# Twelve idle bf16 products around the diagonals in attention's first two turns

## The chip, the cores and the metric

One core of one Trainium2 chip runs the whole program in one launch. The metric is the time on the device in microseconds, the median of several executions. A profiled execution is a further one, with its own time.

## The reference

Three stages follow one another, all in float32:

```
for t in range(S):                       # attention, per batch b and head h
    cur   = (u * k[t]) outer v[t]
    y[t]  = r[t] @ (state + cur)
    state = w[t][:, None] * state + k[t] outer v[t]
x   = y as [1536 tokens, 384]
x   = each token's best expert of 8 (softmax weight, relu(x @ w1[e]) @ w2[e])
out = (silu(x @ w_gate) * (x @ w_val)) @ w_out
```

Batch 2, 8 heads, 768 steps, head size 48; experts 384 to 1024 to 384; the last stage 384 to 1536 to 384.

## The kernel before, in words

Attention is done in chunks of 128 tokens, 12 in all (NU), six for each batch. The loop `for u in range(NU - 2)` at L851 is one turn for each chunk. The program order is written by hand: each engine takes its instructions in the order in which the loop issues them, so what stands ahead on an engine's queue delays what stands behind. For a chunk, VectorE makes scaled keys and queries (prep1 and prep2; tile M at L410 and L413, and rk at L417), TensorE makes the scores (L451), the transposed keys (kgtok, L462), the values y (L474 and L478) and the state's increment (L490), ScalarE copies the results out of PSUM (L453 the scores, L464 the transposed keys as kgt, L509 the state as Sb, L543 the transposed rows and diagonals as xT), and GpSimd masks the scores (L454) and forms the diagonal's part of the output (own, L431). VectorE adds that part to y as x (L515).

In turn u, TensorE's order is: state(u); in turns 0 and 1 some idle products (`warm`); scores(u + 1); kgtok(u + 1); gate_t(u - 1), which has the diagonals and the transposes of the finished chunk's rows; values(u). In turns 0 and 1 gate_t calls `diag`, products with only two moving columns: those of chunks 0 and 1 in turn 0, those of chunk 2 in turn 1. An f32 product counts twice in the profile, so turn 0 has 16 such records and turn 1 has 8. From turn 2 on, the diagonals are made in another form (L531).

`warm(n, pool, tag)` at L435 issues n products of a 128x128 matrix of ones with 512 columns in bf16, to a PSUM buffer of that pool and tag; nobody reads the result. The pool ps1 has one buffer for each tag: "xT" is also gate_t's, "T" is also the buffer of kgtok's transposes (psT), which ScalarE copies out at L464. A new tile of a tag waits until the old one's readers are done. Calls of warm stand ahead of the first scores (12 products), after the first kgtok (4), in turn 0 (8) and in turn 1 (4) ahead of the scores, and at the end of attention (1 and 2).

After the last turns, the tokens are sorted to experts, the first expert's input is formed on TensorE (L795) and the experts begin (L1226, L1244), followed by the last stage (L1337, L1360).

Of the kernel before, what the change touches and what calls it, by code (L numbers as in the profile page):

```python
# [41 lines left out]
def build(tc, cap, dm, tk, vt, ub, cst, wg, w1, w2, wgate, wval, wout, out):  # L42
# [257 lines left out]
    ps1 = at.enter_context(tc.tile_pool(name="ps1", bufs=1, space=PSUM))  # L300
# [51 lines left out]
    def prep1(u):  # L352


        if u >= NU:
            return
        W = dmt[u % 3][:, 0:2 * NP * XW].rearrange("p (h a j) -> p h a j", h=2, a=NP)
        Xf[u] = ap3.tile([128, 2 * (NP * XW + G + 1)], F32, tag="X", name="X")
        X = Xt[u] = halved(Xf[u], XW)
        for h in range(2):  # L360
            nc.vector.tensor_tensor_scan(out=run(X[:, h], h), data0=run(W[:, h], h), data1=run(xinit[:, h], h),
                                         initial=0.0, op0=ALU.mult, op1=ALU.max)
            tick()
        A = halved(anch[u % 2], HC)
        for h in range(2):
            nc.vector.reciprocal(out=anchors(A, h, G - 1), in_=anchors(X, h, G + 1))
            tick()
# [20 lines left out]
    def prep0(u):  # L388

        if u >= NU:  # L390
            return
        W = dmt[u % 3][:, 0:2 * NP * XW].rearrange("p (h a j) -> p h a j", h=2, a=NP)
        m = wm[u % 2].rearrange("p h a (g j) -> p h a g j", j=G)
        w8 = [W[:, h, :, 2 * h:2 * h + HC].rearrange("p a (g j) -> p a g j", j=G) for h in range(2)]
        nc.scalar.copy(out=m[:, 0, :, :, 1:G], in_=w8[0][:, :, :, 0:G - 1])
        nc.scalar.copy(out=m[:, 1, :, :, 0:G - 1], in_=w8[1][:, :, :, 1:G])
# [23 lines left out]
    def diag(u, ps):  # L420

        rk = rkt.pop(u).rearrange("p a s j -> p a (s j)")
        for p in range(NP):
            nc.tensor.matmul(ps[:, 2 * p:2 * p + 2], rk[:, p, :], ud[:, p, E + 2 * p:E + 2 * p + 2], start=True, stop=True)
# [10 lines left out]
    def warm(n, ps=None, tag="T"):  # L435

        ps = (ps or psA).tile([128, 512], F32, tag=tag if ps else "A0", name="psW")
        x = xinit.rearrange("p h a j -> p (h a j)").bitcast(BF16)[:, 0:512]
        for _ in range(n):
            nc.tensor.matmul(ps, ones, x, start=True, stop=True)  # L440

    def scores(u):
        if u >= NU:
            return
        M = Mt[u]
        sb = At[u] = ap2.tile([128, 2, NP, C], F32, tag="A", name="A")
        ps = [psA.tile([128, 512], F32, tag=f"A{g}", name="psA").rearrange("p (a t) -> p a t", a=NP) for g in range(2)]
        for p in range(NP):
            for g in range(2):
                h = M[64 * g:64 * g + 64, p].rearrange("p (x s) b -> p x (s b)", x=2)  # L450
                nc.tensor.matmul(ps[g][:, p], h[:, 0], h[:, 1], start=True, stop=True)  # L451
        for g in range(2):
            nc.scalar.copy(out=sb[:, g], in_=ps[g])  # L453
            nc.gpsimd.affine_select(out=sb[:, g], in_=sb[:, g], pattern=[[0, NP], [1, C]], base=0,  # L454
                                    channel_multiplier=-1, compare_op=ALU.is_gt, fill=0.0)

    def kgtok(u):
        if u < NU and (u + 1) % UPB:
            M = Mt[u]
            pst = ps1.tile([128, NP, C], F32, tag="T", name="psT")  # L460
            for p in range(NP):
                nc.tensor.transpose(pst[:, p, :], M[:, p, 0:2, :].rearrange("p a b -> p (a b)"), ident)  # L462
            kgt[u] = ap2.tile([128, NP, C], F32, tag="kgt", name="kgt")
            nc.scalar.copy(out=kgt[u], in_=pst)  # L464
# [16 lines left out]
    def state(u):  # L481

        if not (u + 1) % UPB:
            return
        P = ps1.tile([128, NP, D], F32, tag="P", name="psP")
        k = kgt.pop(u)
        for p in range(NP):
            for g in range(2):
                c0 = D * (2 * p + g)
                nc.tensor.matmul(P[64 * g:64 * g + 64, p, :], k[:, p, 64 * g:64 * g + 64], vts[u][:, c0:c0 + D],  # L490
                                 start=True, stop=True, skip_group_check=True)
        d = ap2.tile([128, NP], F32, tag="d", name="d")
        nc.vector.tensor_tensor(out=d, in0=Xt[u][:, 1, :, XW - 1], in1=Xt[u + 1][:, 0, :, 0], op=ALU.mult)
        tick()
        src = P
        if u % UPB:
            src = ap2.tile([128, NP, D], F32, tag="Sa", name="Sa")
            nc.vector.tensor_tensor(out=src, in0=P, in1=Sc[u], op=ALU.add)
            tick()
        s = Sc[u + 1] = ap2.tile([128, NP, D], F32, tag="Sc", name="Sc")  # L500
        nc.vector.tensor_tensor(out=s, in0=src, in1=d.unsqueeze(2).to_broadcast([128, NP, D]), op=ALU.mult)
        tick()

    def expand(u):
        if not (u + 1) % UPB:
            return
        s = Sc[u + 1]
        for g in range(2):
            nc.scalar.copy(out=Sb[(u + 1) % 2][64 * g:64 * g + 64, :, D * g:D * g + D], in_=s[64 * g:64 * g + 64])  # L509

    def xrow(u):
        if u < 0:
            return
        x = xt[u] = gp.tile([128, DM], F32, tag="x", name="x", bufs=7)
        nc.vector.tensor_tensor(out=x, in0=yt.pop(u), in1=av.pop(u), op=ALU.add)  # L515
        tick()
# [3 lines left out]
    def gate_t(u, qs=(), rows=()):  # L520


        if u < 0 and not qs:
            return
        ps = ps1.tile([128, 4 * C], F32, tag="T" if u == NU - 1 else "xT", name="psx")
        if rows:
            w, q = rows
            rk = rkt.pop(q).rearrange("p a s j -> p a (s j)")
            todo = [(wgs[:, k, :], xgt[w][:, k, :]) for k in range(3)] + [(ud[:, p, :], rk[:, p, :]) for p in range(NP)]
            for i, (a, b) in enumerate(todo):  # L530
                nc.tensor.matmul(ps[0:2 * E, DM:DM + C], a, b, start=not i, stop=i == len(todo) - 1, skip_group_check=True)  # L531
            gss[u] = gp.tile([2 * E, C], F32, tag="gs", name="gs")
        w = DM + len(qs) * H
        for i, q in enumerate(qs):
            diag(q, ps[:, DM + i * H:])
        for k in range(3 * (u >= 0)):
            nc.tensor.transpose(ps[:, 128 * k:128 * k + 128], xt[u][:, 128 * k:128 * k + 128], ident)
        xT = gp.tile([128, DM + 2 * H], F32, tag="xT", name="xT", bufs=3)
        c0 = 0 if u >= 0 else DM
        if rows:  # L540
            nc.scalar.copy(out=gss[u], in_=ps[0:2 * E, DM:DM + C])
            w = DM
        nc.scalar.copy(out=xT[:, c0:w], in_=ps[:, c0:w])  # L543
        xgt[u] = xT[:, 0:DM].rearrange("p (k c) -> p k c", k=3)
        for i, q in enumerate(qs):
            a8s[q] = xT[:, DM + i * H:DM + i * H + H]
# [169 lines left out]
    def zero(n):  # L716
        for _ in range(min(n, len(zsteps))):
            c, d = zsteps.pop(0)
            nc.sync.dma_start(out=zv[:, c:d], in_=zrow[:, 0:d - c])
# [131 lines left out]
    for u in range(NU - 2):  # L851
        chosen, counted = ended.get(u - 2), ended.get(u - 3)
        xrow(u - 1)
        state(u)
        if u:
            prep0(u + 2)
        if u < 2:
            warm(8 - 4 * u, ps1, "xT")
        scores(u + 1)
        expand(u)  # L860
        kgtok(u + 1)
        if u:
            prep1(u + 2)
        if u >= 2:
            gate_t(u - 1, rows=(u - 2, u + 1))
        else:
            gate_t(u - 1, ((0, 1), (2,))[u])
            if not u:
                own(0)
            own(u + 1)  # L870
        load_dm(u + 4)
        zero(NZ)
        if counted:
            count(counted)
            place(counted)
            ready += counted
        prep2(u + 2)
        if not u:
            check(1)
            nc.vector.tensor_copy(out=tri, in_=before)  # L880
        check(u + 2)
        values(u)
        if u >= 2:
            columns(u - 1, u - 2, u + 1)
            own(u + 1)
        if chosen:
            flush()
            choose(chosen)
        load_v(u + 3)
        if u >= 4:  # L890
            load_raws(2 * (u - 4) + 1)
        if u >= 5:
            fill(0.0)
        for _ in range(2):
            if ready and not steps:
                scatter(ready.pop(0))
# [583 lines left out]
```

## Time and profile before

| what | value |
|---|---|
| median of 3 runs | 479.93 us (479.17 to 482.4) |
| profiled execution | 482.81 us |
| its span, first to last instruction | 481.1 us |
| mean granted TensorE clock in it | 0.974 |
| TensorE / VectorE / ScalarE / GpSimd busy | 97% / 70% / 50% / 15% |

A row of the timeline gives the start, the duration from the first to the last of the merged instructions, the engine, the line, the operation, what is written and read, and the count; in brackets the idle time ahead of it and what ended it. Products overlap at their ends, so the time from one group's start to the next group's start is what a group costs. PE is TensorE's products, PEld its loading of weights, DVE VectorE, ACT ScalarE, POOL GpSimd.

### The profile page before, as it was taken

The numbers are of one execution on the slowest core, as the hardware profiler recorded it, in microseconds if no ns is written. First come the engines' busy times: TensorE is split into PE (matmuls) and PEld (weight loads), VectorE is DVE, ScalarE is ACT, GpSimd is POOL, SyncE is SP. The second block draws the span as 40 slices with busy tenths as digits, with TensorE's granted clock in tenths as the row PEclk, the third lists the DMA queues.
The fourth block names the chain that finished last, engine by engine and source line by source line (L and its number), as shares of the span: only waits on it lengthen the run. The fifth ranks groups of instructions, "written<-read, shape, count | busy, mean of one in ns | idle before, by whom it ended". The sixth has DMA issues, their size and how long they took to land.

```text
span 481.1 us, 8717 instructions
## 1 busy us (share of the span) xinstructions
PE 468.9 (97%) x3268; PEld 423.9 (88%) x3271; DVE 337.4 (70%) x723; ACT 240.8 (50%) x567; POOL 71.7 (15%) x88
## 2 busy tenths in 40 slices
PE   7999999998999999999999999999999999999994
PEld 3798888898999999999998888888888888888884
DVE  8999899756888685568868968475758677433231
ACT  4466666545787677656545454444534434222220
POOL 3343426531000000000000171000000000003033
PEclk9899989958999999999999999999999999999999
DMA  7899994642779964324524244133100000001011
GB/s 239 196 278 257 341 246 154 213 163 74 251 262 376 329 222 146 123 67 138 193 65 118 81 67 68 65 70 128 32 36 1 0 1 0 1 0 65 2 66 65
DMA packets 33647, 62.53 MB, mean 130 GB/s; under 512 B 5216, under 2 KB 16992, under 8 KB 33600
## 3 DMA queue, kind: packets, MB, share of 16 engines
q1 hardware_dynamic: 31680, 57.20, 39.5%
q0 software_dynamic: 1920, 4.73, 2.7%
q8 instruction: 26, 0.43, 0.4%
q14 instruction: 21, 0.17, 0.1%
HBM read 52.48 MB, written 9.44 MB: 129 GB/s over the span
## 4 chain that ended last, share of the span: by engine, by line
PE 72%; issue 2%; POOL 1%; DVE 0%; POOLq 0%
PE psg L1337 31%; PE psu L1360 14%; PE psh L1226 14%; PE pso L1244 13%; POOL out L1372 1%; PE psx L1211 1%; DVE acc L1370 0%; POOLq L1476 0%; POOLq L1372 0%
## 5 line engine op out<-in xcount | busy, mean ns | idle before, releaser
L1337 PE MATMUL psg<-yb,wu 128*128 128x512 f32 x648 | 156.3, 395 | 0.0
L1337 PEld LDWEIGHTS psg<-yb,wu 128*128 128x128 f32 x648 | 121.3, 188 | 26.2
L1360 PE MATMUL psu<-wu,a 128*128 128x384 f32 x432 | 80.8, 336 | 0.0
L1360 PEld LDWEIGHTS psu<-wu,a 128*128 128x128 f32 x432 | 76.4, 188 | 2.9
L1226 PE MATMUL psh<-xe,wu 128*128 128x240 f32 x576 | 69.1, 277 | 1.6 <-ACTq L1165 1.6
L1226 PEld LDWEIGHTS psh<-xe,wu 128*128 128x128 f32 x576 | 66.2, 190 | 1.9 <-ACTq L1165 1.8
L1244 PE MATMUL pso<-h,wu 128*128 128x240 f32 x576 | 66.4, 275 | 0.0
L1244 PEld LDWEIGHTS pso<-h,wu 128*128 128x128 f32 x576 | 65.3, 189 | 0.0
L211 DVE TENSOR_TENSOR wu<-raw,wu 128x512 fp32r<-128x512 f32 x96 | 62.1, 687 | 1.0 <-DVEq L1165 1.0
L1344 DVE TENSOR_TENSOR t<-t,psg 128x512 f32<-128x512 f32 x36 | 24.7, 686 | 52.6 <-PE psg L1337 35.6
L206 ACT CAST wu<-raw 128x512 fp32r<-128x512 f32 x96 | 55.1, 621 | 3.9 <-PE pso L1244 1.8
L1349 ACT CAST a<-t 128x512 fp32r<-128x512 f32 x36 | 22.3, 619 | 58.1 <-DVE t L1344 58.1
L1233 DVE SCALAR_TENSOR_TENSOR h<-psh,h 128x240 fp32r<-128x240 f32 x64 | 25.1, 403 | 22.8 <-ACT h L1232 22.4
L206 ACT CAST wu<-bits 128x384 fp32r<-128x384 f32 x36 | 18.0, 514 | 40.0 <-DVE bits L199 40.0
L1372 POOL DMA_INDIRECT out<-acc,idc x12 | 11.7, 974 | 174.1 <-DVE acc L1370 172.3
L1259 POOL DMA_INDIRECT idl<-ids,dests x12 | 13.5, 1121 | 161.4 <-DVE bits L186 158.0
L1343 ACT ACTIVATE t<-psg 128x512 f32<-128x512 f32 x36 | 21.5, 596 | 27.5 <-PE psg L1337 27.5
L1350 DVE TENSOR_TENSOR a<-t,a 128x512 fp32r<-128x512 f32 x36 | 24.8, 689 | 11.7 <-ACT a L1349 11.7
L478 PE MATMUL y<-v,A 128*128 128x48 f32 x192 | 28.4, 278 | 0.0
L1232 ACT ACTIVATE h<-psh 128x240 fp32r<-128x240 f32 x64 | 23.2, 373 | 9.4 <-PE psh L1226 8.7
L1370 DVE TENSOR_TENSOR acc<-psu,acc 128x384 f32<-128x384 f32 x24 | 12.9, 558 | 20.9 <-PE psu L1360 20.9
L478 PEld LDWEIGHTS y<-v,A 128*128 128x128 f32 x192 | 26.6, 204 | 0.0
(145 smaller groups left out, 584.0 us busy)
## 6 DMA issues: line engine op xcount, KB each, us to landing
raw<-in_moe_w SPq DMA_DIRECT2D x32, 768.0 KB, 6.5
dm<-in_dm SPq DMA_DIRECT2D x18, 291.0 KB, 6.2
scr<-zrow SPq DMA_DIRECT2D x12, 384.0 KB, 5.8
raw<-in_moe_w_gate SPq DMA_DIRECT2D x6, 768.0 KB, 4.4
raw<-in_moe_w_val SPq DMA_DIRECT2D x6, 768.0 KB, 4.5
raw<-in_moe_w_out SPq DMA_DIRECT2D x6, 768.0 KB, 4.4
v<-in_tk SPq DMA_DIRECT2D x12, 192.0 KB, 6.2
dm<-in_dm SPq DMA_DIRECT2D x3, 512.0 KB, 5.7
```

Source lines behind the costliest of these rows:

```text
L206: nc.scalar.copy(out=slot_t[u % NSLOT][:, 0, c:c + n], in_=bits[i])
L211: nc.vector.tensor_tensor(out=w[:, 1, c:c + n], in0=bits.pop(i), in1=R(w[:, 0, c:c + n]), op=ALU.subtract)
L478: nc.tensor.matmul(y[:, c0:c0 + D], A[:, g, p, :], V[:, c0:c0 + D], start=not u % UPB, stop=True, skip_group_check=True)
L1226: nc.tensor.matmul(ps, w[:, a, k, c0:c0 + 128], xet[e][:, b, k, :], start=n == 0, stop=n == 8)
L1232: nc.scalar.activation(out=h[:, 0, :], in_=ps, func=AF.Relu)
L1233: nc.vector.scalar_tensor_tensor(out=h[:, 1, :], in0=ps, scalar=0.0, in1=R(h[:, 0, :]), op0=ALU.max, op1=ALU.subtract)
L1244: nc.tensor.matmul(ypt[e, d], w[:, a, f % 4, 128 * d:128 * d + 128], h[:, b, :], start=f == 0 and n == 0, stop=f == 7 and n == 2)
L1337: nc.tensor.matmul(gps[i][g], w[:, a, g, k, c0:c0 + 128], yb[t, k][:, c], start=a_ == k == 0, stop=a_ == k == 2)
L1344: nc.vector.tensor_tensor(out=t, in0=t, in1=pg[1], op=ALU.mult)
L1349: nc.scalar.copy(out=a[:, 0], in_=t)
L1350: nc.vector.tensor_tensor(out=a[:, 1], in0=t, in1=R(a[:, 0]), op=ALU.subtract)
L1360: nc.tensor.matmul(out_ps[t, j], att[i][:, c, 128 * j:128 * j + 128], w[:, a, f % 4, :], start=f % FP == 0 and n == 0, stop=f % FP == FP - ...
```

## The change

In turns 0 and 1 of the loop at L851, three idle products are issued ahead of gate_t, to the buffer "xT", and three after it, to the buffer "T". Nothing else differs.

```diff
         if u >= 2:
             gate_t(u - 1, rows=(u - 2, u + 1))
         else:
+            warm(3, ps1, "xT")
             gate_t(u - 1, ((0, 1), (2,))[u])
+            warm(3, ps1, "T")
             if not u:
                 own(0)
             own(u + 1)
```

## Rows read from the trace of the kernel before

**Rows 1.** The page: its head, TensorE's share of the span and the chain that ended last, by engine.

```profile
span 481.1 us, 8717 instructions
PE 468.9 (97%) x3268; PEld 423.9 (88%) x3271; DVE 337.4 (70%) x723; ACT 240.8 (50%) x567; POOL 71.7 (15%) x88
...
PE 72%; issue 2%; POOL 1%; DVE 0%; POOLq 0%
```

**Rows 2.** The chain that ended last in order of time (start, duration, what), its first two pieces.

```profile
114.51 0.04 issue
114.55 8.53 PE psh L1226 x72
...
```

**Rows 3.** Busy time of each engine in stretches of the span: length, then busy time and count for each engine, the granted TensorE clock (PEclk) as a share of full speed, the DMA engines' share and GB/s.

```profile
core 0: us, PE busy (x) PEld busy (x) DVE busy (x) ACT busy (x) POOL busy (x), PEclk, DMA share, GB/s
9.00:19.00 10.00, 9.75 (x99) 7.58 (x96) 9.90 (x19) 5.86 (x19) 5.57 (x9) 1.00 0.71 151
19.10:22.40 3.30, 3.08 (x25) 1.82 (x27) 3.27 (x8) 0.58 (x2) 0.56 (x1) 0.50 0.97 199
22.60:24.80 2.20, 2.20 (x27) 2.08 (x26) 2.20 (x6) 1.50 (x4) 0.80 (x2) 1.00 1.11 370
24.80:62.80 38.00, 38.00 (x415) 34.24 (x415) 34.81 (x78) 23.93 (x76) 14.07 (x17) 1.00 0.98 284
63.50:66.80 3.30, 3.30 (x22) 2.68 (x23) 3.27 (x10) 2.49 (x11) 1.34 (x2) 0.50 1.05 314
...
94.20:111.20 17.00, 16.78 (x92) 16.08 (x94) 9.13 (x47) 5.37 (x13) 5.71 (x6) 0.50 0.44 152
111.40:150.00 38.60, 37.02 (x329) 36.70 (x329) 30.88 (x64) 29.50 (x68) 1.95 (x2) 1.00 0.70 232
```

**Rows 4.** Who waited for whom, TensorE from 22 to 94 us (total us, times, longest).

```profile
PE psA L451 <- DVE M L413: 0.4, 1, 0.4
```

**Rows 5.** The same for VectorE from 3.7 to 94 us.

```profile
DVE x L515 <- PE y L478: 3.6, 5, 1.4
DVE t L659 <- PE lg L626: 0.9, 1, 0.9
```

**Rows 6.** The timeline of TensorE's products, from before turn 0 (the first row) through turn 0 (13.78 to 18.97 us), turn 1 and the start of turns 2 and 3.

```profile
10.12 1.03 PE L440 MATMUL psW<-xinit,ones 128*128 128x512 bf16 x4
...
14.88 0.66 PE L462 MATMUL psT<-ident,M 128*128 128x128 f32 x4
15.37 1.84 PE L424 MATMUL psx<-ud,rk 128*128 128x2 f32 x16
17.07 1.96 PE L478 MATMUL y<-v,A 128*128 128x48 f32 x16
18.97 1.03 PE L490 MATMUL psP<-v,kgt 128*64 128x48 f32 x16
19.93 0.61 PE L440 MATMUL psW<-xinit,ones 128*128 128x512 bf16 x1
20.76 1.06 PE L440 MATMUL psW<-xinit,ones 128*128 128x512 bf16 x2 [0.22 <-issue]
21.75 1.50 PE L451 MATMUL psA<-M 64*128 64x128 f32 x16
23.18 0.66 PE L462 MATMUL psT<-ident,M 128*128 128x128 f32 x4
23.68 0.95 PE L424 MATMUL psx<-ud,rk 128*128 128x2 f32 x8
24.49 0.53 PE L537 MATMUL psx<-ident,x 128*128 128x128 f32 x3
24.85 0.36 PE L474 MATMUL y<-Sb,M 128*128 128x96 f32 x2
...
27.56 0.67 PE L490 MATMUL psP<-v,kgt 128*64 128x48 f32 x16
28.16 1.16 PE L451 MATMUL psA<-M 64*128 64x128 f32 x16
29.25 0.66 PE L462 MATMUL psT<-ident,M 128*128 128x128 f32 x4
...
35.48 1.16 PE L451 MATMUL psA<-M 64*128 64x128 f32 x16
```

**Rows 7.** The timeline of ScalarE: the copy of the transposed keys in turn 0, and in turn 1 with the copies ahead of it.

```profile
16.86 0.59 ACT L464 COPY kgt<-psT 128x512 f32<-128x512 f32 x1
...
24.24 0.71 ACT L509 COPY Sb<-Sc 64x192 f32<-64x192 f32 x2
24.98 0.58 ACT L464 COPY kgt<-psT 128x512 f32<-128x512 f32 x1
```

**Rows 8.** The timeline of VectorE: the second half of M of chunk 2 and of chunk 3, and x of chunk 0.

```profile
18.90 1.31 DVE L413 TENSOR_TENSOR M<-dm,R 128x512 f32<-128x512 f32 x1
...
20.87 0.55 DVE L515 TENSOR_TENSOR x<-y,aV 128x384 f32<-128x384 f32 x1
...
26.27 1.31 DVE L413 TENSOR_TENSOR M<-dm,R 128x512 f32<-128x512 f32 x1
```

**Rows 9.** The timeline of TensorE's products further on: the scores of chunk 8, and two groups of the products that form the first expert's input.

```profile
63.46 2.08 PE L451 MATMUL psA<-M 64*128 64x128 f32 x16 [0.37 <-DVE M L413]
...
105.80 2.89 PE L795 MATMUL x<-hot,xhl 128*128 128x240 f32 x12
...
111.38 1.59 PE L795 MATMUL x<-hot,xhl 128*128 128x240 f32 x12
```

**Rows 10.** The idle products' line by itself: count, and the least, median and longest duration of one in ns.

```profile
L440 PE MATMUL psW<-xinit,ones x28: 379/631/634, 3.1 to 104.1; 128*128 128x512 bf16 x28
```

## The prediction

> **What bounds the kernel now.** I read the page first [rows 1]: TensorE is busy in 97% of a span of 481.1 us and the chain that ended last is 72% TensorE. The reader should see that no other engine holds a real share of that chain. The chain in order of time [rows 2] begins at 114.51 us, with the first expert's products, and from there it is TensorE to the end. So everything ahead of 114.5 us counts only by when it lets these products start, and a microsecond lost or won there is one of the total, if nothing between takes it up.
>
> The table of stretches [rows 3] says two things. From 24.8 to 62.8 us TensorE's row is 38.00 of 38.00 us, while VectorE has 34.81: attention's turns are bound by TensorE, VectorE close behind. Its waits agree: five times, 3.6 us in all, VectorE's step x waited for the products y [rows 5], while TensorE waited once, 0.4 us, for VectorE [rows 4]. From turn to turn the scores start at 28.16 and 35.48 us, 7.32 us apart, with no idle time noted between [rows 6]. The second thing is the granted clock: 1.00 up to 19.0, 0.50 from 19.1 to 22.4, then 1.00, 0.50 again from 63.5 to 66.8 and from 94.2 to 111.2, 1.00 after (of the levels 1.2 and 2.4 GHz). TensorE did not stand still ahead of the first fall, but its products were narrow: 16 of 2 columns from 15.37 us, 16 of 48 from 17.07, and the fall comes with the state products at 18.97 [rows 6]. The added products stand around just those 2-column ones.
>
> **The change part by part.** Durations are from the profiled execution: 482.81 us, which is its span of 481.1 and 1.7 around it. That is 2.9 above the median of the runs, 479.93, so I work out a difference and set it on the median.
>
> *Twelve products.* Four of the same kind start at 10.12 us and end 1.03 later at clock 1.00 [rows 6]; the last takes 0.379 by itself, the least that this line shows [rows 10], so one follows another after (1.03 - 0.38) / 3 = 0.217 us. Three cost 0.65 us, twelve 2.60. At clock 0.50 the four of turn 1 (one has no record) take 21.75 - 19.93 = 1.82 us, 0.455 each [rows 6]. So the term lies between 2.60 and 5.46; I take 2.60, since the row at 1.00 is the nearest to where the first six stand, with 3.9 (the first six at 1.00 would be 1.30, six at half 2.73) only if the clock falls early. Their operands, ones and xinit, were written long before. Nothing hides them: TensorE has no idle time in these turns that is not noted above.
>
> *What comes back.* If the clock stays at 1.00 past 19.1 us, the state products take 27.56 to 28.16 = 0.60 us in place of 18.97 to 19.93 = 0.96; the four products that were there already 4 x 0.217 = 0.87 in place of 1.82; the scores 28.16 to 29.25 = 1.09 in place of 21.75 to 23.18 = 1.43 [rows 6]. That is 0.36 + 0.95 + 0.34 = 1.65 us. The bounds are 0 and 1.65. I take all of it: turn 1, whose 2-column products last half as long (23.68 to 24.49) and stand next to transposes and scores, keeps 1.00 [rows 3, 6], and the change cuts turn 0's narrow run in two with wide products.
>
> The Trainium skill speaks against taking it. In "TensorE: Matmul & The Clock Gate", section "Why this matters for your kernels", the advice against a falling clock is to leave TensorE no long idle gap between bursts; by that rule products in a place without a gap would change nothing at the clock, the give-back would be 0 and the time that of the first rival. The trace differs: TensorE's row has 9.75 of the 10 us ahead of the fall, and the clock fell all the same [rows 3].
>
> *New waits.* The first group of each turn writes the buffer that the diagonals write next, only TensorE does both, so there is none. The second group writes the buffer of the transposes of kgtok, which ScalarE copies out. Before, TensorE went on to the diagonals and values without that copy; now everything behind it (values, then the next turn's state and scores) stands behind it, and VectorE's x and ScalarE's copies wait for these. Turn 0: kgtok starts at 14.88 and the diagonals at 15.37; with 0.65 they start at 16.02, take 17.07 - 15.37 = 1.70, and TensorE comes to the second group at 17.72. The copy lasts from 16.86 to 17.45 [rows 7]: no wait. Turn 1: values of turn 0 start at 18.37 and take 18.97 - 17.07 = 1.90, so 20.27; state 0.60, four products 0.87, so the scores start at 21.74 (the M that they need was done at 18.90 + 1.31 = 20.21 [rows 8]); 1.09 for them, 0.50 for kgtok, 0.65, 0.81 for the diagonals, 0.36 for the transposes: 25.19. ScalarE's copy ended at 24.98 + 0.58 = 25.56 [rows 7] with scores that started their successor at 23.18; now that is 22.83, so it ends at 25.21. A wait of about 0.05. Its bounds are 0 and 0.4 (the copy not earlier); I take 0.05. This cover is thin: the copy stands behind two others on ScalarE, at 24.24 [rows 7], and each tenth that those come later is a tenth here.
>
> *Other queues.* ScalarE's copy of the diagonals in turn 0, and with it GpSimd's product for x, come 0.65 later; x starts at 20.87 behind VectorE's own work [rows 8] and needs the y that is now done at 20.27, so nothing waits. No DMA moves.
>
> *Sum.* 2.60 - 1.65 + 0.05 = +1.0 us: values of turn 1 start at 25.85 in place of 24.85. It is not made up later. The only place where TensorE waits for VectorE, 0.4 us at 63.46 us [rows 4, 9], is behind a VectorE wait of 0.9 for counts from TensorE [rows 5], so it moves along. At the scores of turn 2 there was slack for VectorE, not TensorE: their M was done at 26.27 + 1.31 = 27.58 [rows 8] and they started at 28.16 [rows 6]. So 479.93 + 1.0 = 480.9 (the profiled execution 483.8).
>
> **The rivals.**
> *The clock falls all the same*, or the shorter narrow run ends in another fall. For it: TensorE's 16 narrow products of 48 columns remain in one piece, and the fall came at their end. Against: turn 1. Then the 2.60 stays whole: 479.93 + 2.6 = 482.5.
>
> *A later low stretch goes.* All that follows stands 1.0 us later, and the places at 63.5 and 94.2 may fall elsewhere. For it: the median is 2.9 below the profiled execution and the runs shown go from 479.17 to 482.4, so not every execution has all three in full. The second lasts 3.3 us at half, worth at most 1.65 where TensorE is full; VectorE is as full there (3.27 of 3.3 [rows 3]), which holds some back. 480.9 - 1.6 = 479.3, a hair faster than before. Against: nothing near those places is edited.
>
> *Slower: the third stretch lasts longer.* It ended at 111.3 us, with the last products for the first expert's input at full speed: 12 records in 1.59 us at 111.38, while 12 such took 2.89 at 105.80 [rows 9]. If the shift lets the clock stay at 0.50 there, it costs 1.3 us, and as TensorE then stands still until 114.5, the expert's first products would start low; another 3.3 us at half costs 1.7. That is 480.9 + 3.0 = 483.9. It decides if the clock is 0.50 at 112 us. Against: TensorE has wide products from 105.80 on, which the shift leaves in order.
>
> *VectorE hides it.* It has 9.90 of 10 us up to 19 us [rows 3]; were it the bound, TensorE's additions would be free: 479.9. Against: its waits for y [rows 5] and the 0.6 us of slack for M at 28.16.
>
> **How the numbers follow.** Forecast 480.9: 0.55. Clock falls all the same, 482.5: 0.17. A later stretch goes, 479.3: 0.17. Third stretch longer, 483.9: 0.08. VectorE hides it: 0.03. One per cent is 4.8 us, about what a measurement of this kernel can tell from no change. None of the cases passes it alone: slower by more takes the longer third stretch with a remaining fall, 479.93 + 2.6 + 3.0 = 485.5, and unlucky runs, 0.06; faster by more takes all three stretches shortened, 0.02; within, 0.92. The range goes from 477.8 (a second low stretch's 1.6 on top of the 479.3) to 484.4 (the longer third stretch with the 0.4 of the wait).
>
> **What would show it.** Right: the clock's row at 19 to 23 us is 1.00; in turn 0 three products before the diagonals, three after with no idle time ahead; scores of turn 1 (the ones at 21.75) at their old start and 0.3 shorter; values of turn 1 about 1.0 us later and the scores at 28.16 near 29.2; the expert's first product near 115.5. Wrong: 0.50 still in that row; a wait for ScalarE's copy of some tenths ahead of the second groups; the scores at 28.16 unmoved, which would say that VectorE is the bound; or a low stretch of other length after 60 us, which would outweigh all of the sum.

## The result

The changed kernel took 486.12 us (median of 4 runs, 484.65 to 486.26), before 481.13 (4 runs: the three behind the 479.93 that the forecast was set on, and one at 482.33); the ratio is 1.0105, with a 95% interval from 1.0062 to 1.0149. The forecast of 480.9, within 477.8 to 484.4, was wrong: the change costs time, and the four runs lie above the range. Four later executions of the same kernel had a median of 485.77, and twelve still later ones 483.98 beside 480.35 for before, ratio 1.0058 (1.0027 to 1.0089); that last median lies inside the range. One execution of either kernel differs from the next by several microseconds, so part of the first result is the executions, and what follows takes the two apart. A ratio leaves out executions that lie more than 1.5% above the fastest of their kernel, while medians and means hold all of them. The profiled execution: 486.26 us, span 484.5.

The stretches of the changed kernel's span, columns as in [rows 3]:

```profile
core 0: us, PE busy (x) PEld busy (x) DVE busy (x) ACT busy (x) POOL busy (x), PEclk, DMA share, GB/s
9.00:19.00 10.00, 9.69 (x90) 6.68 (x89) 9.90 (x20) 5.11 (x14) 4.50 (x8) 1.00 0.69 167
19.40:26.00 6.60, 6.38 (x43) 5.03 (x45) 5.39 (x12) 0.98 (x6) 1.60 (x2) 0.50 1.01 343
26.30:62.80 36.50, 36.44 (x382) 32.15 (x379) 30.02 (x61) 21.32 (x69) 13.29 (x15) 1.00 0.77 233
63.50:66.80 3.30, 3.30 (x38) 3.00 (x36) 2.37 (x13) 2.71 (x8) 1.23 (x2) 1.00 1.07 266
...
97.90:114.80 16.90, 16.68 (x94) 15.98 (x95) 9.30 (x48) 5.37 (x13) 5.40 (x6) 0.50 0.44 150
```

The clock still falls at 19.3 us, and stays at 0.50 until 26.1, twice as long as in [rows 3]. The stretch at 63.5 us is gone, the third is as it was. TensorE's timeline answers to [rows 6]:

```profile
13.88 1.16 PE L451 MATMUL psA<-M 64*128 64x128 f32 x16
14.98 0.66 PE L462 MATMUL psT<-ident,M 128*128 128x128 f32 x4
15.47 0.81 PE L440 MATMUL psW<-xinit,ones 128*128 128x512 bf16 x3
16.34 1.95 PE L424 MATMUL psx<-ud,rk 128*128 128x2 f32 x16
18.15 0.81 PE L440 MATMUL psW<-xinit,ones 128*128 128x512 bf16 x3
18.79 3.02 PE L478 MATMUL y<-v,A 128*128 128x48 f32 x16
21.74 1.10 PE L490 MATMUL psP<-v,kgt 128*64 128x48 f32 x16
22.77 0.61 PE L440 MATMUL psW<-xinit,ones 128*128 128x512 bf16 x1
...
24.58 1.88 PE L451 MATMUL psA<-M 64*128 64x128 f32 x16
26.39 0.65 PE L462 MATMUL psT<-ident,M 128*128 128x128 f32 x4
26.88 0.81 PE L440 MATMUL psW<-xinit,ones 128*128 128x512 bf16 x3
27.75 1.05 PE L424 MATMUL psx<-ud,rk 128*128 128x2 f32 x8
...
29.03 0.81 PE L440 MATMUL psW<-xinit,ones 128*128 128x512 bf16 x3
29.68 0.36 PE L474 MATMUL y<-Sb,M 128*128 128x96 f32 x2
...
32.38 0.67 PE L490 MATMUL psP<-v,kgt 128*64 128x48 f32 x16
32.98 1.16 PE L451 MATMUL psA<-M 64*128 64x128 f32 x16
```

The scores of chunk 1 before:

```profile
13.78 1.16 PE L451 MATMUL psA<-M 64*128 64x128 f32 x16
```

From the scores of chunk 1 (13.88 us here, 13.78 before) to those of chunk 3 (32.98 and 28.16) it took 19.10 us in place of 14.38, so 4.72 more. Read by start to start: the groups behind gate_t cost 0.64 and 0.65, as worked out; those ahead of the diagonals 0.87 and 0.87, and the diagonals 0.11 more in each turn. Values of turn 0, at half clock now, take 2.95 in place of 1.90, the scores of turn 1 take 1.81 in place of 1.43, the state 0.07 more. 0.64 + 0.65 + 0.87 + 0.87 + 0.22 = 3.25 for the products, 1.05 + 0.38 + 0.07 = 1.50 for the clock. Of the scores' 4.8 us at 32.98, 1.5 come back where the second stretch was; the first expert's product starts at 117.94, 3.4 us later:

```profile
117.94 8.54 PE psh L1228 x72
```

Why 0.87 and not 0.65 is in the timeline of TensorE's weight loads, in which the bracket is the idle time ahead:

```profile
16.34 1.86 PEld L424 LDWEIGHTS psx<-ud,rk 128*128 128x128 f32 x16 [0.55 <-PE psW L440]
...
27.75 0.97 PEld L424 LDWEIGHTS psx<-ud,rk 128*128 128x128 f32 x8 [0.55 <-PE psW L440]
```

The diagonals' first weights wait 0.55 us for the three products to end, since both groups write one PSUM buffer (the run with another buffer, below, tests that). TensorE waits for itself, 0.33 us in each turn by start to start (0.22 ahead of the diagonals, 0.11 in them).

### The profile page after: what moved, and what is told of

Its sections match the earlier page's. It is cut to its first block, busy times and chain, and to the rows that moved or that the text cites. A ratio compares the mean times of both kernels' runs of the same rounds, so it can differ in the third digit from the quotient of the medians.

```text
span 484.5 us, 8739 instructions
## 1 busy us (share of the span) xinstructions
PE 472.2 (97%) x3280; PEld 425.8 (88%) x3283; DVE 336.3 (69%) x723; ACT 240.9 (50%) x567; POOL 73.0 (15%) x88
## 4 chain that ended last, share of the span: by engine, by line
PE 72%; issue 2%; POOL 1%; DVE 0%; POOLq 0%
PE psg L1339 30%; PE psu L1362 14%; PE psh L1228 13%; PE pso L1246 13%; POOL out L1374 1%; PE psx L1213 1%; DVE acc L1372 0%; POOLq L1478 0%; POOLq L1374 0%
## 5 line engine op out<-in xcount | busy, mean ns | idle before, releaser
L206 ACT CAST wu<-bits 128x384 fp32r<-128x384 f32 x36 | 18.0, 514 | 40.0 <-DVE bits L199 38.7
L478 PE MATMUL y<-v,A 128*128 128x48 f32 x192 | 29.4, 285 | 0.0
L478 PEld LDWEIGHTS y<-v,A 128*128 128x128 f32 x192 | 27.8, 211 | 0.1
```

The costliest lines, as they stand in the source:

```text
L206: nc.scalar.copy(out=slot_t[u % NSLOT][:, 0, c:c + n], in_=bits[i])
L478: nc.tensor.matmul(y[:, c0:c0 + D], A[:, g, p, :], V[:, c0:c0 + D], start=not u % UPB, stop=True, skip_group_check=True)
```

## The experiments

Executions of one kernel differ in how long TensorE stood at 0.50. Each run lists span and mean clock, so the time at 0.50 is 2 x (1 - clock) x span; I call it low time. (The clock is listed to 0.001, so low time is known to half a microsecond.) Over all runs, with one line for each kernel and one common slope, a time rises by 0.42 us for each us of low time; the distance between two lines is the price at equal low time, "above" in the table, with its 95% interval. The fit takes low time to cost the same wherever it falls, which nobody tested. It can be seen without a fit: at a mean clock of 0.981 before had 479.95 to 480.33 and the change 483.01; at 0.978 before had 480.07 to 481.31 and the change 482.87 to 484.01. In the table the change and before have the runs of all sessions whose clock is listed.

| kernel | runs | mean us | low time us | above, us |
|---|---|---|---|---|
| before | 110 | 480.38 | 19.4 | 0 |
| the change | 20 | 484.66 | 23.0 | 2.7 ± 0.3 |
| e1_turn0 | 10 | 483.29 | 23.1 | 1.3 ± 0.4 |
| e2_turn1 | 7 | 482.87 | 23.9 | 0.6 ± 0.5 |
| e3_ahead0 | 10 | 483.32 | 24.4 | 0.8 ± 0.4 |
| e5_split | 10 | 482.51 | 25.3 | -0.4 ± 0.4 |
| e6_fewer | 4 | 486.89 | 33.5 | 0.5 ± 0.6 |
| e7_inside | 10 | 480.83 | 19.9 | 0.2 ± 0.4 |
| e8_later | 5 | 484.57 | 23.0 | 2.7 ± 0.5 |
| e9_other_buffer | 11 | 483.15 | 20.2 | 2.4 ± 0.4 |
| e10_moved | 11 | 481.58 | 22.5 | -0.1 ± 0.4 |
| e11_dose | 6 | 481.25 | 17.1 | 1.8 ± 0.5 |
| f1_tail_before | 12 | 477.84 | 9.5 | 1.6 ± 0.4 |
| f2_tail_after | 12 | 480.45 | 9.0 | 4.5 ± 0.4 |
| f3_tail_moved | 12 | 480.10 | 14.6 | 1.7 ± 0.4 |

**Before once more.** No edit.

> The kernel before once more, for its low stretches of the granted clock. Theory A (what the products are decides when the clock falls): a low stretch from about 19.1 us of some 3.4 us, as in the first profile. Rival B (chance: each execution has its own): the first fall is elsewhere or missing, by a microsecond or more. The second stretch at 63.5 us is open in both: the runs between 479.2 and 482.4 us say that something of some 3 us differs between executions.

```profile
17.40:24.10 6.70, 6.70 (x47) 4.91 (x45) 6.67 (x14) 2.18 (x12) 2.17 (x2) 0.50 0.99 269
...
99.30:106.00 6.70, 6.70 (x42) 5.94 (x43) 4.03 (x21) 2.83 (x6) 1.94 (x2) 0.50 0.58 199
```

478.72 us. The fall is again at the values of turn 0 (in them here, right behind them before) but 1.8 us earlier, the first stretch is twice as long, the second missing, the third 6.8 us in place of 17. Both theories were half right: in these two traces the clock falls beside the same products, while the moment and the length differ from one execution to the next. The Trainium skill says on the page "TensorE: Matmul & The Clock Gate", section "Part 1: The HAM clock gate (the "warmup" mystery)", that the same kernel has 6, 11 or 14 products at the low clock in different runs. It says so of the rise at a kernel's start; what differs between these two traces is a fall, at 17.3 us here against 19.1.

**The change once more, twice.** No edit.

> The changed kernel once more, for more executions. Seen so far: with the mean granted clock of each run, times of one kernel fall on a line (some 0.4 us for each us at 0.50), the changed kernel lies 3.7 us above before at the same mean clock, and its four runs had 24 us at 0.50 against 19 for before. Theory A (the change itself brings more low time): again some 5 us more low time than before and a median of 485 to 486.5. Rival B (the four runs happened to fall low): low time about 19 us, median 482.5 to 484.

> The changed kernel in more executions beside as many of before. If its long third stretch was the luck of eight executions: some of its runs now lie at 482 to 484 us with a mean clock of 0.980 or more, like the short ones of before, and its mean comes to 483.5 to 485. If the change always has it: nearly all runs at 485.5 to 486.3 us and a mean clock of 0.973 or 0.974, and 5.5 us above before.

r1_after had 485.77 us (4 runs, ratio 1.0131, 1.0078 to 1.0185), as its theory A expected; r2_after had 483.98 (12 runs, 480.39 to 486.2), with a mean of 483.89, inside the 483.5 to 485 expected if the long stretch was luck. The stretches of the first:

```profile
18.00:28.10 10.10, 10.10 (x60) 7.82 (x59) 8.07 (x17) 2.88 (x13) 2.86 (x3) 0.50 1.00 258
...
99.90:113.40 13.50, 13.50 (x79) 12.65 (x79) 7.63 (x40) 5.37 (x13) 4.68 (x5) 0.50 0.48 163
```

and of the second:

```profile
18.20:24.90 6.70, 6.48 (x37) 5.03 (x36) 4.78 (x9) 1.77 (x10) 2.48 (x2) 0.50 0.98 230
...
100.10:113.60 13.50, 13.10 (x76) 12.34 (x76) 8.87 (x45) 4.52 (x10) 3.33 (x4) 0.50 0.44 150
```

The clock fell in turn 0 in all three traces of the change. The first eight executions all had 22 to 26 us of low time, which the twelve did not repeat (14 to 26, 21.6 on average): part of the first result's excess is these executions. Not all of it: over the 20 runs low time is 3.7 ± 1.7 us above that of before.

**Parts of the change.** Turn 0's six alone (`if not u:` ahead of both new calls), turn 1's six alone (`if u:`), and turn 0's first three alone:

```diff
+            if not u:
+                warm(3, ps1, "xT")
             gate_t(u - 1, ((0, 1), (2,))[u])
```

> Only turn 0's six products. Theory A (the products push the narrow products of values of turn 0 into the low stretch, which then lasts about 6.8 us in place of 3.4): clock 0.50 from about 19.3 to 26.1 us, scores of turn 2 some 3.3 us later than before (1.3 for the six, 1.1 for values at half clock, 0.9 for what else stands at half), time 2 to 4 us above before. Rival B (a plain price of 0.217 us for each product, the longer low stretch being chance): scores of turn 2 1.3 us later and the time 1.3 above before.

> Only turn 1's six products. Theory A: the first low stretch stays as before, 19.1 to 22.5 us, and the six cost their plain 1.3 us, so the scores of turn 2 start 1.3 us later; time 1.3 above before, unless the later low stretch at 63.5 us goes (then 0.2 below). Rival C (the wait for ScalarE's copy ahead of the second group): idle time ahead of that group and 1.5 us or more.

> Only turn 0's three products ahead of the diagonals. Theory A: the narrow run behind them is as long as before and starts 0.65 us later, so the clock falls at about 19.2 us in the midst of values (18.0 to 19.9), and the stretch lasts 3.4 or 6.8 us according to how much of values is left in it; scores of turn 2 0.65 to 2.2 us later. Rival B: 0.65 us later, stretch of 3.4 us.

Medians 482.81, 482.79 and 484.62 us; ratios 1.0066 (1.003 to 1.0102), 1.0067 (1.0048 to 1.0087) and 1.0069 (1.0027 to 1.0111). Scores of chunk 1 to scores of chunk 3 took 19.24, 15.98 and 13.80 us, with first low stretches of 10.2 us, 3.4 and none. For the first two theory A fits the trace, but e2 had as much low time as e1 although its turn 0 is that of before, and that theory A can't explain. e3's trace met neither of its expectations: with three products added the clock did not fall in turn 0, and the interval is 0.58 us shorter than before's 14.38. No wait ahead of the second group appeared in e2, so rival C falls.

**Twelve products in turns 3 and 4**, at the same places around gate_t (`if u in (3, 4):`).

> The same twelve products at the same two places of gate_t, but in turns 3 and 4, where no 2-column products stand and where the clock was 1.00 in every trace; turns 0 and 1 as before. Theory A (what is above the plain price comes from turn 0's narrow products): plain price with the self-wait, 2.6 to 3.3 us, and low time as before (19.4 us on average), so a median of 482.5 to 483.5. Rival G (any added work raises the low time, by moving all that follows): low time 23 to 25 us and 485 to 486 as the change.

Median 485.44 us (5 runs), ratio 1.0112 (1.0081 to 1.0142): 2.7 above at equal low time, as theory A expected, but with low time of 23 us and a median as rival G expected. The price doesn't hang on turn 0's narrow products, and neither does the extra low time.

**The first group to another buffer.**

```diff
-            warm(3, ps1, "xT")
+            warm(3, ps1, "lg")
             gate_t(u - 1, ((0, 1), (2,))[u])
             warm(3, ps1, "T")
```

> The change with the first group of each turn written to a buffer that the diagonals don't use (that of the logits, idle until turn 2). Seen in the changed kernel's trace: the load of the diagonals' weights stands idle 0.55 us until the three products have ended, because both write one buffer; from the products' start to the diagonals' start it takes 0.87 us and not 0.65, and the diagonals take 0.11 more. Theory F (a wait of TensorE for itself): that idle time goes, products to diagonals 0.65 us, 0.33 us less in each turn, 0.66 less at the same mean clock. Rival: the 0.87 is the price of wide bf16 products after f32 ones, and it stays. The time itself: 485 to 486 by A, since the low time is not touched.

```profile
13.06 1.16 PE L451 MATMUL psA<-M 64*128 64x128 f32 x16
...
14.65 0.81 PE L440 MATMUL psW<-xinit,ones 128*128 128x512 bf16 x3
15.30 1.84 PE L424 MATMUL psx<-ud,rk 128*128 128x2 f32 x16
17.49 0.81 PE L440 MATMUL psW<-xinit,ones 128*128 128x512 bf16 x3 [0.35 <-ACT kgt L464]
18.14 1.88 PE L478 MATMUL y<-v,A 128*128 128x48 f32 x16
...
29.00 1.16 PE L451 MATMUL psA<-M 64*128 64x128 f32 x16
```

Products to diagonals 0.65 us, and the diagonals' load no longer waits: theory F holds in the trace. But nearly all of the 0.66 us comes back as a wait of the second groups for ScalarE's copy, by start to start 0.49 us in turn 0 and 0.13 in turn 1. TensorE reached the second group of turn 0 1.15 us earlier than in the changed kernel's trace (0.82 of that was there already at the scores of chunk 1), and the copy still ended at 17.45 us. So the twelve cost 3.20 us in this trace, beside 3.25. At equal low time e9 lies 2.4 above before, 0.3 ± 0.4 less than the change, which can't tell 0 from 0.66. Median 482.89, ratio 1.006 (1.0029 to 1.0091).

The trace shows one thing more. Six products stand in turn 0 as in the change, and here the clock stayed at 1.00 through both turns:

```profile
9.00:28.00 19.00, 18.35 (x167) 14.24 (x169) 18.56 (x33) 10.54 (x33) 8.56 (x12) 1.00 0.79 228
```

From the scores of chunk 1 to those of chunk 3 it took 15.94 us, 1.56 more than before's 14.38. That is the 3.20 less 1.65, the prediction's give-back at its full size, in one execution.

**More, or elsewhere.** Six and six in turn 0 alone (buffer "lg"); six in turn 0 inside the narrow runs; and, with no product added, turn 1's four moved there (2 and 2, `warm(8, ...)` of turn 0 kept):

```diff
         for i, q in enumerate(qs):
+            if i:
+                warm(3, ps1, "lg")
             diag(q, ps[:, DM + i * H:])
...
-        values(u)
+        if u:
+            values(u)
+        else:
+            values(u, range(2))
+            warm(3, ps1, "lg")
+            values(u, range(2, NP))
```

> Twelve products in turn 0 alone, six ahead of the diagonals and six behind, to the buffer that nobody waits for. Theory A with enough wide work: the clock stays at 1.00 through turn 0 in most executions, so the low time falls to 13 to 17 us, and 2.6 for the products less some 2 for the clock gives 480 to 482. Rival H (no number of products around the diagonals holds the clock): first low stretch of 6.8 us or more, 485 or above.

> Six products in turn 0 as in the run with turn 0's six alone, but placed inside the narrow runs: three between the diagonals of chunk 0 and chunk 1, three in the middle of values of turn 0, to a buffer that nobody reads. Theory A (the length of a narrow run decides): the first low stretch goes, price 1.3 us, time 479.5 to 481.5 and less low time than the 23 us of turn 0's six around the diagonals. Rival E (the share of wide work over the whole turn decides, not its place): low time and time as with turn 0's six, 482.8.

> No product added against before: turn 1's four go, and two stand between the diagonals of turn 0 and two inside values of turn 0. Theory A (placed inside the narrow runs they shorten the low stretch): low time as before or less, time 478 to 480. Rival I (turn 1's four are what brings the clock back after a fall): the first low stretch lasts 10 us or more, and the time is 482 or above.

With twelve in one turn, this stretch of e11_dose has the clock at 1.00 throughout:

```profile
9.00:28.00 19.00, 18.70 (x175) 14.49 (x173) 18.39 (x33) 10.52 (x33) 8.89 (x12) 1.00 0.84 193
```

481.89 us, ratio 1.0035 (0.9993 to 1.0078), and 17.1 us of low time, close to theory A's 13 to 17 and 480 to 482. At equal low time the twelve cost 1.8 us; what is left of that in the ratio is not clear of noise. With six inside the runs, the clock still falls in the trace, which theory A did not expect:

```profile
18.20:24.80 6.60, 6.60 (x40) 4.39 (x40) 5.67 (x12) 1.56 (x9) 1.83 (x2) 0.50 1.04 256
```

but the median is 480.3, ratio 0.9994 (0.9952 to 1.0036), so six there cost nothing that can be measured while six around the diagonals cost 0.7%. The trace by itself does show their price: its scores of chunk 1 to chunk 3 took 17.11 us, 1.2 more than r0_before's 15.91 with a low stretch of the same 6.8 us. Why the runs show less is not shown. Moved: 480.9, ratio 1.0012 (0.9983 to 1.0042), with runs from 476.8 to 489.8; neither side of its expectation. In its trace, too, the clock stayed up through both turns, and there VectorE became the bound ahead of chunk 3's scores:

```profile
26.84 1.16 PE L451 MATMUL psA<-M 64*128 64x128 f32 x16 [1.10 <-DVE M L413]
```

So where the clock stays up, some of the time of added products can fall into a wait that is there without them. Whether that is why several prices at equal low time lie below 0.217 us for each product was not tested.

**Without before's twelve**, and **the diagonals of chunk 1 in turn 1**:

> The twelve idle products that before has in turns 0 and 1 (8 and 4, ahead of the scores) are left out. Theory A (every idle product in these turns stands on the path and costs its 0.217 us): 2.6 us less at the same mean clock, and the low time says what they are worth: if it grows by under 6 us, this kernel is faster than before. Rival D (they hide under VectorE): no change at the same clock, only the loss by a lower clock, so 480 to 483.

> No product added: the diagonals of chunk 1 move from turn 0 to turn 1, so that turn 0 has 8 records of 2 columns and turn 1 has 16. TensorE's work is the same. Theory A (the long narrow run of turn 0, 16 records of 2 columns and then 16 of 48, brings the first fall): the first low stretch goes or is shorter in turn 0 and may appear in turn 1; time 0 to 2 us below before if it goes. Rival B (falls come by chance of the execution, not by that run): first stretch and time as before, 479.6.

```profile
14.90:38.70 23.80, 23.80 (x149) 22.34 (x148) 16.68 (x35) 10.29 (x33) 7.24 (x9) 0.50 0.86 229
```

e6_fewer: 486.01 us, ratio 1.0159 (1.0091 to 1.0227). Low from 14.9 to 38.7 us in the trace, and 33.5 us of low time over the four runs: without the products that were there the kernel loses more than they cost. At equal low time nothing was gained (0.5 ± 0.6), as rival D expected, and in the trace TensorE then waited 1.84 us for VectorE's M ahead of the scores in turn 0, so the eight products there hid under VectorE. The time of 486 lies above rival D's 480 to 483, by the low time. e5_split: 480.95, ratio 1.0056 (1.0012 to 1.0099), with the first stretch of 3.4 us still in turn 0 and low time of 25.3. Both are misses for theory A.

**Without the long third stretch.** Eleven more idle products at the end of attention, in before, in the change, and in the moved version:

```diff
+    warm(3)
     values(u, range(2))
...
+    warm(3)
     logits(u - 1)
...
-    warm(1)
+    warm(3)
     values(u + 1, range(2))
...
+    warm(3)
     values(u + 1, range(2, NP))
```

> Before with eleven more idle products at the end of attention: three ahead of the first values of the chunk before the last, three ahead of its logits, three in place of one ahead of the last chunk's values, three in the middle of them. If wide products hold the clock there too, the third low stretch is 0 to 7 us in place of 7 to 17 and the low time falls from 19 to about 8 us; 2.4 us for the products less some 4 gives 478 to 480. If they don't: 482.

> The change with the same eleven products. Theory A (the extra low time is the first stretch's): 3.1 us at equal clock plus 4 to 6 us more low time than f1_tail_before, so 5 to 5.7 us above it, as without the eleven. Rival J (the extra low time was the third stretch's, moved by what stands ahead): no more low time than f1_tail_before, so 3.1 us above it.

> The kernel with turn 1's four products moved into turn 0's narrow runs, and the same eleven at the end. If both help: the lowest low time of all, under 8 us, and 476 to 479, faster than before and the change. Its executions without the eleven had 480 to 490 us in the low cases, so a spread of several us may remain.

Of f1_tail_before:

```profile
18.10:24.70 6.60, 6.38 (x45) 4.81 (x46) 6.57 (x14) 2.51 (x11) 2.05 (x3) 0.50 1.04 266
25.00:110.00 85.00, 82.34 (x860) 73.43 (x862) 73.47 (x199) 52.30 (x158) 37.61 (x43) 1.00 0.77 232
110.30:113.50 3.20, 3.20 (x17) 3.20 (x17) 1.41 (x3) 1.25 (x3) 0.82 (x1) 0.50 0.36 125
```

and of f2_tail_after:

```profile
17.50:27.60 10.10, 9.88 (x57) 7.67 (x58) 7.87 (x16) 2.65 (x13) 2.62 (x2) 0.50 0.93 308
27.80:110.00 82.20, 81.30 (x849) 71.91 (x849) 69.02 (x185) 50.29 (x153) 36.13 (x42) 1.00 0.74 220
```

Behind the first stretch the clock stays at 1.00 up to 110 us in both, and low time falls to 9.5 and 9.0 us on average. The change then costs 480.45 - 477.84 = 2.6 ± 1.6 us, with no more low time: rival J. f2_tail_after had a median of 480.58, ratio 0.9998 (0.9963 to 1.0033). And f1_tail_before has the lowest mean of all, with a median of 478.25 us against 479.98, ratio 0.9931 (0.9897 to 0.9965), as expected: idle products pay at the end of attention, where the low stretch lasted 6.8 to 17.1 us in the traces without them, and not around these diagonals. f3_tail_moved had 479.01 and missed its expectation of under 8 us of low time (14.6). Its ratio is 0.9936 (0.9899 to 0.9972), but five of its twelve runs lie at 483.3 to 484.0, and the mean of all twelve is not clear of that of before (-0.3 ± 1.9 us).

## Why the prediction was wrong

**Twelve products, 2.60: right.** The groups that wait for nobody take 0.64 to 0.65 us for three.

**New waits, the first group: wrong.** "The first group of each turn writes the buffer that the diagonals write next, only TensorE does both, so there is none." The weight loads' rows show 0.55 us of idle time, 0.33 us by start to start, twice, in every trace of the change; e9's other buffer takes it away. The sum put this term at nothing. Products and self-wait are 2.60 + 0.66 = 3.26, against 2.7 ± 0.3 at equal low time over 20 runs and 2.6 to 2.9 in the pair without the third stretch; what hides the remaining 0.5 is open.

**New waits, the second group: nearly right.** There is no idle time ahead of it in either turn of the result's trace. In the three later traces of the change the group of turn 0 starts 0.04 to 0.05 us after ScalarE's copy ends, and the diagonals take 1.97 us up to it in place of 1.81, a wait of 0.16. The cover is thin, as said: in e9 these waits were 0.49 and 0.13.

**What comes back, 1.65: wrong, and this is the step that made a price into "no change".** The clock did not stay at 1.00: in all three traces of the change (four with f2) it fell in turn 0, and values ran at half speed; in the result's trace that cost 1.50 us where 1.65 was to come back. In the four traces whose turns 0 and 1 are before's (before, r0, e8, f1) the first stretch lasted 3.4, 6.8, 3.4 and 6.8 us, in the four of the change 6.8, 10.2, 6.8 and 10.2; chunk 1's to chunk 3's scores took 14.3 to 15.9 us there, 19.1 to 20.9 here. Those are single executions, though: over twelve runs each, f1 and f2 had the same low time (a difference of -0.6 ± 3.2 us), which at 0.42 gives a give-back of 0.2 ± 1.4 us. So no give-back is seen; that this stretch makes it negative on average is not shown. The inference from turn 1, where the clock stayed up beside 8 narrow records, did not carry over to turn 0 with 16 and then 16 more. Nor does the number of products settle it: the clock stayed up in turn 0 in the traces of e11 with twelve there, of e9 with six and of e3 with three, and fell in those of the change, e1 and e7 with six. The size of 1.65 was right where it came, in e9's trace; taking it as the sure case was not.

**The Trainium skill's rule on idle gaps** ("TensorE: Matmul & The Clock Gate", section "Why this matters for your kernels"), weighed in the prediction: with 9.69 of 10 us busy the clock fell, so the trace goes against it again; but its consequence, that nothing comes back, fits the traces of the change. The first rival, at 482.5, had the right mechanism, and with the self-wait it would have read 483.2. The case added up to 485.5 came nearest to the result by luck: it takes a longer third stretch, and that one lasted 16.9 us, as before.

**Passing on to the end: right.** In the result's trace TensorE was the bound: no idle time between turns, VectorE's waits for y grew from 3.6 to 6.6 us in the window of [rows 5], and the one TensorE wait for M was again 0.4:

```profile
DVE x L515 <- PE y L478: 6.6, 5, 3.9
```

**The range.** It took no account of the executions. Before alone runs from 477.8 to 484.1 with how long its stretches last, so the median of four runs can stand a microsecond or two off. With both wrong terms set right, 3.26 us on 479.93 gives 483.2, still within the range. What carried the result out of it is the low time of its four runs, 24.4 us against 19.4 on average in before, worth some 2.1 us. The sum had no term for that, though the prediction named a low stretch of other length after 60 us as a sign of being wrong. Over 20 executions the mean is 484.66, 4.27 above before, of which 2.72 at equal low time and (23.05 - 19.40) x 0.424 = 1.55 by low time.

**Slips in the sums**, which don't move the forecast: 21.74 + 1.09 + 0.50 + 0.65 + 0.81 + 0.36 is 25.15 and not 25.19 (the wait of 0.05 fits 25.15), 1.30 + 2.73 is 4.0 and not 3.9, and the ends of the range come to 477.7 and 484.3.

**What stays open.** Why five kernels that add work or move it (e1, e2, e3, e5, e8) had 23 to 25 us of low time in their 5 to 10 runs. The cause of the change's own 3.7 us more, 1.55 us of the miss, stays open with it. With the third stretch mostly taken away the difference in low time between the change and before is gone, which points there; whether the added work really lengthens that stretch, or these few executions fell so, the runs don't say. Open, too, is what decides in an execution whether the clock falls in turn 0.

## What to carry to other kernels

Idle products on an engine that is the bound cost most of their price (2.7 of 3.3 us here), and give it back only if the clock in fact stays up; count that as a case, not as the forecast, until traces of several executions show it. A product group that takes over another's PSUM buffer can make TensorE wait for itself, so give it a buffer of its own, and look what the next wait is: here it took back nearly all of the gain. Where executions differ in their time at half clock, compare kernels at equal mean clock, and look for the longest low stretch first: here it was the last one, and filling that made the kernel faster.

## What the runs showed of the hardware

Two groups of TensorE's products that write one PSUM buffer are enough for a wait: 0.55 us ahead of a weight load, and none with a buffer of its own (e9). The granted clock fell with TensorE busy 9.69 of 10 us, after products of 2 and 48 columns, and in e6's trace it stood at 0.50 for 23.8 us with TensorE busy 23.80 of 23.80. The time at 0.50 differed between executions of one program from 12 to 28 us (mean clocks of before from 0.987 to 0.971), and their times by some 6 us.
